# On-chip casts of the first high halves, a mask built in two parts, and constant matmuls in the early gaps of TensorE

## The chip, the cores and the metric

The kernel runs on one core of one Trainium2 chip. The metric is the device time of one execution in microseconds (us); lower is better. The engines are named as the profile names them: PE (TensorE, matmul), PEld (its weight loads), DVE (VectorE), ACT (ScalarE), POOL (GpSimd) and SP (SyncE, here only a queue that issues DMAs). PEq, ACTq, SPq and so on are the sequencers of the engines.

## The reference

Block-sparse attention over 4 batches, 8 heads, 768 positions and a head size of 64, followed by a layer norm and a two-layer feed-forward network with a residual:

```python
scores = scale * np.matmul(q, k.transpose(0, 1, 3, 2))
mask = np.abs(blk_i - blk_j) <= window          # blocks of 32 positions
mask = mask | (blk_i == 0) | (blk_j == 0) | (blk_i == n_blocks - 1) | (blk_j == n_blocks - 1)
for qb in range(n_blocks):
    for kb in sampled_blocks[qb]:                # three random blocks for each block of queries
        mask[qb * block:(qb + 1) * block, kb * block:(kb + 1) * block] = True
scores = np.where(mask, scores, -1000000000.0)
attn = np.exp(scores - np.max(scores, axis=-1, keepdims=True))
attn = attn / (np.sum(attn, axis=-1, keepdims=True) + 1e-09)
x = np.matmul(attn, v)                           # heads side by side: (4, 768, 512)
xn = (x - mu) / np.sqrt(var + 1e-06) * g_ln
out = x + np.maximum(xn @ w_ch1, 0.0) @ w_ch2    # 512 -> 2048 -> 512
```

## The kernel before

**Numbers in two halves.** An operand of a matmul that must be exact to about float32 is kept as two float16 tiles: a high half, which is the value rounded to float16, and a low half, which is the float32 value minus the high half. A product is then three float16 matmuls (high by high, low by high, high by low). For k and q the float32 original is loaded by a DMA issued on SP into `raw` (k) or `qr` (q). The high half `kh` or `qh` comes from a second DMA of the same data that converts to float16 on the way and is issued on POOL. The low half `kl` or `ql` is a subtraction: on DVE for the first k and the first q, on POOL for all the others.

**Units, segments, slots.** A unit is one batch and 256 of its 768 queries: 12 units. Each has 4 segments (pairs of heads), so there are 48 segments, each with one q load; and 16 k loads, one for each batch and pair of heads. A segment has 4 slots (2 tiles of 128 queries by 2 heads). A pair of slots is scored together: 12 float16 matmuls into two `ps` tiles (line 475). Then DVE adds the mask and takes the row extreme (`masked_max`, line 484, which reads the mask `allow`), ACT takes the exponential (line 498), and the result `p` is transposed. In the first 8 segments ("early") PE transposes it against `ident` into one of three PSUM tiles `bank` (line 512), ACT and DVE copy it to `pt` (line 519), and the product with v is made in float32 (line 588). In the other 40 segments ACT and DVE make two halves `ph` and `pl`, DMAs transpose them, and the product is in float16 (lines 592 and 597). After four segments comes the layer norm of the unit and then its feed-forward matmuls (lines 754 and 835), which work with both halves and use the same `bank` tiles.

**Weights.** The network's weights arrive as float64 bits. DVE takes three integer passes over each piece (lines 423, 427 and 431), ACT scales it and makes the high half (lines 458 and 460), POOL the low half (line 461). There are 8 pieces of the first layer (128x1024) and 16 of the second (128x512).

**The mask.** `allow` holds, for each of the 6 tiles of 128 queries, one number for each of 24 blocks of keys, and a seventh row with the block numbers. It and the sampled blocks (`samp_i`) are loaded by DMAs issued on ACT. `build_mask` is one cast, three pairs of compare and maximum, and one scaling, each over all 6 tiles (128x144 elements), all on DVE. Unit c of a batch reads tiles 2c and 2c+1.

**The planner.** The order of instructions on every engine is computed before the kernel is built. `Plan.add` records a task with its engine, a cost in ns, the tasks that it follows, a rank and the ring places that it takes or gives back. `Plan.run` plays the tasks through a list scheduler: a clock for each engine, `bus` for the DMA engines (a transfer occupies it for `load` ns), `lock` for DVE and POOL work that is kept apart, and a state `warm` for PE, in which a matmul costs its planned time, against 1.9 times that while it is not warm. Before, PE counts as warm after 4200 ns without an idle stretch over 2500 ns. A task is emitted when it is picked, so the picks are the program order of each engine. On the chip each engine works through its own list in order and waits only for the data of the next instruction. A changed cost anywhere can change the order of everything that follows. The tasks of the feed-forward matmuls have the last rank, so they fill whatever PE time attention leaves.

Of the kernel before, what the change touches and what calls it, by code (L numbers as in the profile page):

```python
# [10 lines left out]
F16 = mybir.dt.float16  # L11
# [3 lines left out]
ALU = mybir.AluOpType  # L15

NEG = -(2.0**40)
# [8 lines left out]
class Plan:  # L26
# [7 lines left out]
    LOOK = 120  # L34

    def __init__(self):
        self.tasks, self.rings, self.sets = [], {}, {}
# [7 lines left out]
    def add(self, engine, cost, emit, after=(), rank=0.0, more=100, take=(), give=(), lock=False,  # L45
            mode=None, load=None, order=None, slack=0):
        t = SimpleNamespace(engine=engine, cost=cost, emit=emit, rank=rank, more=more, take=take,
                            give=give, lock=lock, mode=mode, load=load, n=len(self.tasks),
                            after=[x for x in after if x is not None], end=None, left=0, next=[],
                            order=order, slack=slack)  # L50
# [38 lines left out]
    def where(self, name, owner):  # L89
        return (self.rings.get(name) or self.sets[name]).at[owner]  # L90

    def run(self):
        clock = dict.fromkeys(("PE", "DVE", "ACT", "POOL", "SP"), 0.0)
        held = {"DVE": 0.0, "POOL": 0.0}
        ready = {e: [t for t in self.tasks if t.engine == e and not t.left] for e in clock}
        bus, mode, done, warm, since = 0.0, None, 0, False, 0.0
        while done < len(self.tasks):
            best = None
            for e, now in clock.items():
                pick = None  # L100
                for t in ready[e]:
                    start = max([now] + [x.free if x.engine == "PE" == e or x.order == t.order
                                         and x.order else x.end + (t.slack if x.engine != e else 0)
                                         for x in t.after])
# [9 lines left out]
                    key = (max(start, now + self.LOOK), t.rank, t.n)  # L114
                    if pick is None or key < pick[0]:
                        pick = (key, start, t)
                if pick and (best is None or pick[1] < best[1]):
                    best = pick
            assert best, ("stuck", done, [(e, [(x.rank, x.take) for x in v][:6])
                                          for e, v in ready.items()])  # L120
            _, start, t = best
            ready[t.engine].remove(t)
            cost = t.cost
            if t.engine == "PE":
                if t.mode != mode:
                    start += 90
                mode = t.mode
                if start - clock["PE"] > self.idle:
                    warm, since = False, start
                warm = warm or start - since > self.heat  # L130
                if not warm:
                    cost *= 1.9
            t.free = clock[t.engine] = start + cost
# [7 lines left out]
            for name, owner in t.give:  # L141
                r = self.rings.get(name) or self.sets[name]
# [15 lines left out]
def sparse_attention_moe(  # L158
# [12 lines left out]
    nc = tc.nc  # L171
    P = 128
    B, NPAIR, NCH, _, CH = qs.shape
# [3 lines left out]
    NB = blocks.shape[2]  # L177
    NR = sampled.shape[2]
    BLK = S // NB
    KT = S // P  # L180
# [4 lines left out]
    TS = CH // P  # L185
# [4 lines left out]
    EARLYLN = 1  # L190
    EASY, EASE = 34, (0, 1500, 500)
    PORC = ()
    W1POS = (2.0, 2.0)
    W2POS = (16.0, 1.0)

# [10 lines left out]
    op = ctx.enter_context(tc.tile_pool(name="op", bufs=2))  # L206
# [4 lines left out]
    ctx.enter_context(tc.manual_schedule(engines={ET.SP, ET.Pool, ET.DVE, ET.Activation}))  # L211

    plan = Plan()
    plan.idle, plan.heat, plan.deep = 2500.0, 4200.0, 7000.0
    for name, size in (("k", 4), ("v", 4), ("vr", 2), ("q", NQ), ("qr", 3), ("ps", 2), ("p", 4),
                       ("ph", 2), ("pl", 2), ("pt", 5), ("pa", 1), ("xT", 3), ("xh", 1),
                       ("hh", 1), ("hl", 1), ("ln", 1), ("ot", 2)):
# [14 lines left out]
    eps = const.tile([P, 1], F32, name="eps")  # L232
    nc.vector.memset(eps, 1e-6)
    allow = const.tile([P, KT + 1, NB], F32, name="allow")
    nc.scalar.dma_start(allow, blocks)
    samp_i = const.tile([P, KT, 2 * NR], I32, name="samp_i")
    nc.scalar.dma_start(samp_i, sampled.bitcast(I32))
    g_sb = const.tile([P, CT], F32, name="g_sb")
    nc.scalar.add_instruction(
        mybir.InstLoadActFuncSet(  # L240
# [10 lines left out]
    w1v = w1.rearrange("(c p) f -> p c f", p=P)  # L251
    w2f, w2g = (x.rearrange("p f e -> p (f e)") for x in (w2h, w2l))

    def build_mask():
        nc.vector.tensor_copy(samp_f, samp_i.rearrange("p c (r t) -> p c r t", t=2)[:, :, :, 0])
        hit = w1h[:, CT - 1, DF - 2 * KT * NB :].bitcast(F32).rearrange("p (t n) -> p t n", n=NB)
        ids = allow[:, KT : KT + 1, :].to_broadcast([P, KT, NB])
        for r in range(NR):
            nc.vector.tensor_tensor(out=hit, in0=ids,
                                    in1=samp_f[:, :, r : r + 1].to_broadcast([P, KT, NB]),  # L260
                                    op=ALU.is_equal)
            nc.vector.tensor_tensor(out=allow[:, 0:KT], in0=allow[:, 0:KT], in1=hit, op=ALU.max)
        nc.vector.tensor_scalar(out=allow[:, 0:KT], in0=allow[:, 0:KT], scalar1=-NEG,
                                scalar2=NEG, op0=ALU.mult, op1=ALU.add)

    units, segs, slots = [], [], []
# [17 lines left out]
    def loads_k(b, pr, rank, before):  # L284
        idx = b * NPAIR + pr
# [8 lines left out]
        def low():  # L294
# [1 line left out]

        o.raw = plan.add("SP", 580, raw, (before,), rank, 1400, load=1120, order="k",
                         take=(("k", idx), ("raw", ("k", idx), 1, RAWS)))
        o.high = plan.add("POOL", 560, lambda: nc.gpsimd.dma_start(o.kh, ks[b, pr]), (o.raw,),
                          rank, 2300, load=1100, order="k")  # L300
        e, c = ("POOL", 1640) if idx else ("DVE", 960)
        o.low = plan.add(e, c, low, (o.raw, o.high), rank, give=(("raw", ("k", idx)),), lock=True)
        return o
# [1 line left out]
    def loads_q(n, rank, before):  # L305
# [3 lines left out]
        def raw():  # L309
# [7 lines left out]
        o.high = plan.add("POOL", 560, lambda: nc.gpsimd.dma_start(o.qh, qs[u.b, pr, u.c]),  # L317
                          (o.raw,), rank, 2300, load=400, order="q")
        e, c = ("POOL", 660) if n else ("DVE", 650)
        o.low = plan.add(e, c, lambda: (nc.gpsimd if n else nc.vector).tensor_sub(  # L320
            o.ql, o.qr, o.qh), (o.raw, o.high), rank, give=(("qr", n),), lock=True)
        return o
# [571 lines left out]
    for seg in segs:  # L894
# [4 lines left out]
        for t in range(TS):  # L899
# [105 lines left out]
```

## Time and profile before

| what | value |
|---|---|
| time before, median of 3 runs (lowest, highest) | 816.51 us (814.61, 822.39) |
| the profiled execution: its own time | 817.7 us |
| its span, first to last instruction | 815.9 us |
| PE busy | 779.8 us (96%) |
| DVE, ACT, POOL busy | 610.9, 514.9, 173.9 us |
| granted PE clock, mean | 0.987 |
| first score matmul; first feed-forward matmul | 7.29 us; 92.5 us |

The span is read in two stretches: the head, up to the first feed-forward matmul, in which PE waits for other engines again and again, and the rest, in which it hardly waits at all. "Idle before" in a row is the time that an engine stood still just before that instruction, with the releaser that ended it.

### The profile page before, as it was taken

The page shows a single profiled execution, that of the slowest core. Times are in us where ns is not written, and L with a number is a line of the kernel's source. Part 1 is how long each engine was busy: PE and PEld are TensorE (multiplying, and loading weights), DVE is VectorE, ACT ScalarE, POOL GpSimd, SP SyncE. Part 2 cuts the span into 40 slices and gives each one's busy share as a digit, 9 for nine tenths or more (in the row PEclk, how much of TensorE's full clock was granted, in tenths as well). Part 3 has the DMA queues.
Part 4 walks back from the last instruction along what each step waited for, and adds up shares of the span by engine and source line. Part 5 has one row for each costly group of instructions (what it writes and reads, how often), then busy time and mean ns, then how long its engine had stood idle before and what let it go on. Part 6 is the DMA issues. An engine that isn't in the chain of part 4 may idle for free.

```text
span 815.9 us, 18386 instructions
## 1 busy us (share of the span) xinstructions
PE 779.8 (96%) x7228; PEld 592.4 (73%) x7228; DVE 610.9 (75%) x1203; ACT 514.9 (63%) x942; POOL 173.9 (21%) x188
## 2 busy tenths in 40 slices
PE   4787899999999999999899999999999999999998
PEld 2454567777777867777677777777777777788887
DVE  5899988968988878868878778868869778745120
ACT  2778788668686666677666666668766656723020
POOL 4635454413211012143111012332100100000000
PEclk9799899999999999999999999999999999999999
DMA  9853424899989779999678699899697585750000
GB/s 283 289 174 95 132 70 116 159 159 207 168 155 141 130 136 168 160 193 173 124 136 141 107 152 174 168 181 169 131 144 142 107 150 101 115 107 2 27 2 27
DMA packets 293383, 112.49 MB, mean 138 GB/s; under 512 B 260400, under 2 KB 285104, under 8 KB 293296
## 3 DMA queue, kind: packets, MB, share of 16 engines
q1 hardware_dynamic: 283792, 104.91, 64.1%
q0 software_dynamic: 9216, 6.30, 6.2%
q8 instruction: 57, 0.93, 0.5%
q14 instruction: 30, 0.25, 0.1%
q10 hardware_dynamic: 288, 0.10, 0.1%
HBM read 48.34 MB, written 6.29 MB: 67 GB/s over the span
## 4 chain that ended last, share of the span: by engine, by line
PE 77%; DVE 11%; DMA 5%; ACT 4%; issue 1%; SPq 1%; ACTq 0%; DVEq 0%
PE bank L835 28%; PE bank L754 26%; PE ps L475 10%; PE pa L592 6%; DMA pt<-pl 3%; PE pa L597 3%; DVE p L484 2%; PE pa L588 2%; DVE pl L553 2%; PE bank L512 1%; ACT p L498 1%; DMA pt<-ph 1%; DVE w2h L427 1%; DMA samp_i<-sampled 1%; DMA raw<-w 1%
## 5 line engine op out<-in xcount | busy, mean ns | idle before, releaser
L498 ACT ACTIVATE p<-p,st 128x768 f32<-128x768 f32 x192 | 177.8, 926 | 43.4 <-DVE st L484 41.9
L549 ACT ACTIVATE ph<-p,st 128x768 f16<-128x768 f32 x160 | 145.3, 929 | 92.2 <-DVE st L540 42.0
L835 PE MATMUL bank<-hh,w2h 128*128 128x256 f16 x704 | 192.3, 273 | 2.5 <-DVE xc L685 2.5
L553 DVE SCALAR_TENSOR_TENSOR pl<-p,st,ph 128x768 f16<-128x768 f32 x160 | 164.3, 1038 | 38.9 <-DMA pt<-pl 37.4
L484 DVE CUSTOM_DVE_ANT_1 p<-ps,allow 128x768 f32<-128x768 f32 x192 | 178.4, 947 | 18.5 <-PE ps L475 17.4
L835 PE MATMUL bank<-hl,w2h 128*128 128x256 f16 x704 | 191.9, 273 | 0.0
L835 PE MATMUL bank<-hh,w2l 128*128 128x256 f16 x704 | 191.9, 273 | 0.0
L754 PEld LDWEIGHTS <-w1h 128*128 128x128 f16 x1536 | 146.9, 98 | 27.6 <-issue 10.7
L835 PEld LDWEIGHTS <-w2h 128*128 128x128 f16 x1408 | 134.5, 98 | 27.4 <-issue 12.4
L754 PE MATMUL bank<-xl,w1h 128*128 128x256 f16 x768 | 115.8, 274 | 0.0
L754 PE MATMUL bank<-xh,w1l 128*128 128x256 f16 x768 | 115.7, 273 | 0.0
L754 PE MATMUL bank<-xh,w1h 128*128 128x256 f16 x768 | 115.4, 273 | 0.1
L769 ACT ACTIVATE hh<-bank 128x512 f16<-128x512 f32 x96 | 56.6, 590 | 80.9 <-PE bank L754 80.2
L775 DVE SCALAR_TENSOR_TENSOR hl<-bank,hh 128x512 f16<-128x512 f32 x96 | 65.9, 686 | 35.4 <-ACT hh L769 35.1
L475 PE MATMUL ps<-kh,qh 64*128 64x256 f16 (+1 forms) x384 | 72.2, 338 | 14.2 <-DMA qh<-q 7.3
L592 PE MATMUL pa<-pt,vh 128*64 128x512 f16 x480 | 82.1, 383 | 0.7 <-issue 0.6
L754 PEld LDWEIGHTS <-w1l 128*128 128x128 f16 x768 | 73.9, 98 | 12.1 <-issue 3.8
L475 PEld LDWEIGHTS <-qh 64*128 64x128 f16 x768 | 32.5, 96 | 62.6 <-issue 28.2
L835 PEld LDWEIGHTS <-w2l 128*128 128x128 f16 x704 | 68.9, 98 | 8.0
L475 PE MATMUL ps<-kl,qh 64*128 64x256 f16 (+1 forms) x384 | 69.7, 334 | 1.4 <-DVE kl L295 1.4
L475 PE MATMUL ps<-kh,ql 64*128 64x256 f16 (+1 forms) x384 | 68.3, 334 | 1.2 <-DVE ql L320 1.2
L597 PE MATMUL pa<-pt,vl 128*64 128x256 f16 x480 | 67.4, 273 | 0.0
(106 smaller groups left out, 921.7 us busy)
## 6 DMA issues: line engine op xcount, KB each, us to landing
raw<-k SPq DMA_DIRECT2D x16, 384.0 KB, 4.6
qr<-q SPq DMA_DIRECT2D x48, 128.0 KB, 3.3
raw<-w SPq DMA_DIRECT2D x12, 512.0 KB, 3.6
out<-ot SPq DMA_DIRECT2D x48, 128.0 KB, 2.0
vr<-v SPq DMA_DIRECT2D x24, 192.0 KB, 2.9
w2l<-w SPq DMA_DIRECT2D x4, 1024.0 KB, 9.6
kh<-k POOLq DMA_DIRECT2D x16, 192.0 KB, 5.2
qh<-q POOLq DMA_DIRECT2D x48, 64.0 KB, 3.5
```

The source lines that it names most:

```text
L475: nc.tensor.matmul(s.ps[:, lo:hi], x[rows, s.qs], y[rows, lo:hi], start=n == 0, stop=n == len(terms) - 1)
L484: nc.vector.tensor_tensor_reduce(out=s.p.rearrange(blk, k=BLK), in0=s.ps[:, 0:S].rearrange(blk, k=BLK), in1=bias, scale=-0.125, scalar=3.0 ...
L498: nc.scalar.activation(s.p, s.p, AF.Exp, bias=s.st[:, j : j + 1], scale=-1.0, accum_out=total)
L549: nc.scalar.activation(s.ph, s.p, AF.Copy, scale=s.r)
L553: nc.vector.scalar_tensor_tensor(out=s.pl, in0=s.p, scalar=s.r, in1=s.ph, op0=ALU.mult, op1=ALU.subtract)
L588: nc.tensor.matmul(seg.pa[half[hh], 0:CH], vo.whole(hh)[:, t, :], pts[keys[hh]][:, t, :], start=t == 0, stop=t == KT - 1, skip_group_check ...
L592: nc.tensor.matmul(seg.pa[half[hh], 0 : 2 * CH], vo.vh[:, hh, t, :], pts[keys[hh]][:, t].rearrange("p i n -> p (i n)"), start=t == 0, stop ...
L597: nc.tensor.matmul(seg.pa[half[hh], 0:CH], vo.vl[:, hh, t, :], pts[keys[hh]][:, t, 0, :], start=False, stop=t == KT - 1, skip_group_check= ...
L754: nc.tensor.matmul(dst, w[:, ct, fs], x[:, ct, :], start=n == 0 and ct == 0, stop=n == 2 and ct == CT - 1, skip_group_check=True)
L769: nc.scalar.activation(u.hh[:, f : f + 2, :].rearrange("p f n -> p (f n)"), bank[plan.where("bank", own)], AF.Relu)
L775: nc.vector.scalar_tensor_tensor(out=u.hl[:, f : f + 2, :].rearrange("p f n -> p (f n)"), in0=bank[plan.where("bank", own)], scalar=0.0, i ...
L835: nc.tensor.matmul(dst, w[:, k, e * P : (e + 1) * P], x[:, k, :], start=k == 0 and n == 0, stop=k == FT - 1 and n == 2)
```

## The change

1. **High halves cast on chip.** For the first four k loads and the first four q loads the converting DMA on POOL is gone. The high half is now a copy from the float32 tile: on ACT for the k loads and for q loads 1 to 3, on DVE for q load 0. The planned cost of the DVE subtraction for `ql` of load 0 goes from 650 to 350 ns.
2. **The mask in two parts.** `build_mask(lo, hi)` works on a range of tiles. Part one covers tiles 0 and 1 and is a DVE task of rank 0 that is not picked before 5400 ns of the plan; part two covers tiles 2 to 5, rank 6, not before 12000 ns. A slot of the first unit of a batch waits for part one, all others for part two. `samp_i` is loaded before `allow`.
3. **Matmuls on constants.** When the planner picks a PE task that starts before 60 us of the plan, and PE's clock stands before that start, it takes the `bank` tile that comes free first and emits as many matmuls of `ones_h` by a constant (128x128 weights, 256 columns) as fit in the gap less 300 ns, counted at 115 ns each while it holds PE for warm and at 220 ns while not; under 4 it emits none. Nothing reads their result.
4. **The planner's picture of the chip.** The clocks start at 700 ns instead of 0 and `bus` at 1800 ns. PE is warm when it was busy for more than 85% of the last 3400 ns, and stays so while that is over 40%.

```diff
+    def fill(self, now, start, each):
+        free = self.sets["bank"].free
+        place = min((p for p in free if free[p] is not None), key=lambda p: free[p], default=None)
+        begin = max(now, self.first, free[place] if place is not None else start)
+        count = int((start - begin - 300) // each)
+        if count >= 4:
+            self.filler(place, count)
+            free[place] = begin + each * count + 200
+            self.work.append((begin, begin + each * count))
...
-        clock = dict.fromkeys(("PE", "DVE", "ACT", "POOL", "SP"), 0.0)
+        clock = dict.fromkeys(("PE", "DVE", "ACT", "POOL", "SP"), 700.0)
...
-        bus, mode, done, warm, since = 0.0, None, 0, False, 0.0
+        bus, mode, done, warm = 1800.0, None, 0, False
...
+            if t.engine == "PE" and start < self.keep:
+                self.fill(clock["PE"], start, 115 if warm else 220)
...
-                if start - clock["PE"] > self.idle:
-                    warm, since = False, start
-                warm = warm or start - since > self.heat
+                part = sum(max(0, b - max(a, start - self.span)) for a, b in self.work[-60:])
+                part /= self.span
+                warm = part > self.hot or warm and part > self.cold
...
+    KEEP = 60e3
+    CASTK, CASTQ = 4, 4
...
-    plan.idle, plan.heat, plan.deep = 2500.0, 4200.0, 7000.0
+    plan.span, plan.hot, plan.cold, plan.deep = 3400.0, 0.85, 0.4, 7000.0
+    plan.keep, plan.first = KEEP, 1400.0
...
-    nc.scalar.dma_start(allow, blocks)
     samp_i = const.tile([P, KT, 2 * NR], I32, name="samp_i")
     nc.scalar.dma_start(samp_i, sampled.bitcast(I32))
+    nc.scalar.dma_start(allow, blocks)
...
+    def filler(place, count):
+        for _ in range(count):
+            nc.tensor.matmul(bank[place][:, 0 : 2 * P], ones_h, ones.bitcast(F16), start=True,
+                             stop=True)
...
-    def build_mask():
+    def build_mask(lo, hi):
+        ts, n = slice(lo, hi), hi - lo
...
-        o.high = plan.add("POOL", 560, lambda: nc.gpsimd.dma_start(o.kh, ks[b, pr]), (o.raw,),
-                          rank, 2300, load=1100, order="k")
+        if idx < CASTK:
+            o.high = plan.add("ACT", 900, lambda: nc.scalar.copy(o.kh, o.kr), (o.raw,), rank)
+        else:
+            o.high = plan.add("POOL", 560, lambda: nc.gpsimd.dma_start(o.kh, ks[b, pr]),
+                              (o.raw,), rank, 2300, load=1100, order="k")
...
+        if n < CASTQ:
+            o.high = plan.add("ACT" if n else "DVE", 310 if n else 200, lambda: (
+                nc.scalar.copy if n else nc.vector.tensor_copy)(o.qh, o.qr), (o.raw,), rank)
...
-    mask = plan.add("DVE", 2300, build_mask, (), -2000, 100)
-    mask.more = 4000
+    masks = [plan.add("DVE", 1250, lambda: build_mask(0, TS), (), 0, 100),
+             plan.add("DVE", 2100, lambda: build_mask(TS, KT), (), 6, 100)]
+    masks[0].wake, masks[1].wake = 5400.0, 12000.0
...
-                last_m = plan.add("DVE", 880, lambda s=s: masked_max(s), (sc, mask, last_m),
+                last_m = plan.add("DVE", 880, lambda s=s: masked_max(s), (sc, masks[u.c > 0], last_m),
```

More of the change, by code (lines that the diff above doesn't have):

```diff
@@ L36, in __init__ @@
     def __init__(self):
-        self.tasks, self.rings, self.sets = [], {}, {}
+        self.tasks, self.rings, self.sets, self.work = [], {}, {}, []
     def ring(self, name, size):
@@ L49, in add @@
                             after=[x for x in after if x is not None], end=None, left=0, next=[],
-                            order=order, slack=slack)
+                            order=order, slack=slack, wake=0.0)
         for x in t.after:
@@ L101, in run @@
                 for t in ready[e]:
-                    start = max([now] + [x.free if x.engine == "PE" == e or x.order == t.order
+                    start = max([t.wake] + [x.free if x.engine == "PE" == e or x.order == t.order
                                          and x.order else x.end + (t.slack if x.engine != e else 0)
@@ L114, in run @@
                     key = (max(start, now + self.LOOK), t.rank, t.n)
+                    start = max(start, now)
                     if pick is None or key < pick[0]:
@@ L127, in run @@
                 mode = t.mode
-                if start - clock["PE"] > self.idle:
-                    warm, since = False, start
-                warm = warm or start - since > self.heat
+                part = sum(max(0, b - max(a, start - self.span)) for a, b in self.work[-60:])
+                part /= self.span
+                warm = part > self.hot or warm and part > self.cold
                 if not warm:
                     cost *= 1.9
+                self.work.append((start, start + cost))
             t.free = clock[t.engine] = start + cost
@@ L252, in sparse_attention_moe @@
     w2f, w2g = (x.rearrange("p f e -> p (f e)") for x in (w2h, w2l))
-    def build_mask():
-        nc.vector.tensor_copy(samp_f, samp_i.rearrange("p c (r t) -> p c r t", t=2)[:, :, :, 0])
+    def filler(place, count):
+        for _ in range(count):
+            nc.tensor.matmul(bank[place][:, 0 : 2 * P], ones_h, ones.bitcast(F16), start=True,
+                             stop=True)
+    plan.filler = filler
+    def build_mask(lo, hi):
+        ts, n = slice(lo, hi), hi - lo
+        nc.vector.tensor_copy(samp_f[:, ts],
+                              samp_i.rearrange("p c (r t) -> p c r t", t=2)[:, ts, :, 0])
         hit = w1h[:, CT - 1, DF - 2 * KT * NB :].bitcast(F32).rearrange("p (t n) -> p t n", n=NB)
-        ids = allow[:, KT : KT + 1, :].to_broadcast([P, KT, NB])
+        hit = hit[:, ts]
+        ids = allow[:, KT : KT + 1, :].to_broadcast([P, n, NB])
         for r in range(NR):
             nc.vector.tensor_tensor(out=hit, in0=ids,
-                                    in1=samp_f[:, :, r : r + 1].to_broadcast([P, KT, NB]),
+                                    in1=samp_f[:, ts, r : r + 1].to_broadcast([P, n, NB]),
                                     op=ALU.is_equal)
-            nc.vector.tensor_tensor(out=allow[:, 0:KT], in0=allow[:, 0:KT], in1=hit, op=ALU.max)
-        nc.vector.tensor_scalar(out=allow[:, 0:KT], in0=allow[:, 0:KT], scalar1=-NEG,
+            nc.vector.tensor_tensor(out=allow[:, ts], in0=allow[:, ts], in1=hit, op=ALU.max)
+        nc.vector.tensor_scalar(out=allow[:, ts], in0=allow[:, ts], scalar1=-NEG,
                                 scalar2=NEG, op0=ALU.mult, op1=ALU.add)
@@ L316, in loads_q @@
                          take=(("q", n), ("qr", n)))
-        o.high = plan.add("POOL", 560, lambda: nc.gpsimd.dma_start(o.qh, qs[u.b, pr, u.c]),
-                          (o.raw,), rank, 2300, load=400, order="q")
-        e, c = ("POOL", 660) if n else ("DVE", 650)
+        if n < CASTQ:
+            o.high = plan.add("ACT" if n else "DVE", 310 if n else 200, lambda: (
+                nc.scalar.copy if n else nc.vector.tensor_copy)(o.qh, o.qr), (o.raw,), rank)
+        else:
+            o.high = plan.add("POOL", 560, lambda: nc.gpsimd.dma_start(o.qh, qs[u.b, pr, u.c]),
+                              (o.raw,), rank, 2300, load=400, order="q")
+        e, c = ("POOL", 660) if n else ("DVE", 350)
         o.low = plan.add(e, c, lambda: (nc.gpsimd if n else nc.vector).tensor_sub(
```

## The prediction

> **What bounds the kernel now.** I read first the slices of the page, then the busy time of each engine by stretch, cut at the events that matter: first matmul, first masked maximum, the end of the loaded DMA stretch, 60 us (where the constant matmuls stop), and the first feed-forward matmul.
>
> ```profile
> PEclk9799899999999999999999999999999999999999
> DMA  9853424899989779999678699899697585750000
> ```
> ```profile
> 0.00:7.28 7.28, 0.00 (x0) 0.00 (x0) 1.62 (x8) 1.28 (x1) 3.55 (x11) 1.00 0.81 211
> 7.28:12.31 5.03, 2.46 (x12) 0.81 (x13) 3.59 (x6) 0.00 (x0) 3.54 (x4) 1.00 1.08 295
> 12.31:35.00 22.69, 17.48 (x102) 10.60 (x101) 18.37 (x29) 13.11 (x22) 10.30 (x9) 0.77 1.05 340
> 35.00:60.00 25.00, 20.97 (x161) 12.40 (x159) 23.19 (x45) 20.48 (x37) 11.77 (x10) 0.93 0.51 168
> 60.00:92.40 32.40, 25.27 (x190) 15.68 (x186) 28.96 (x59) 26.16 (x53) 15.79 (x11) 0.95 0.38 115
> 92.40:110.00 17.60, 15.95 (x133) 10.96 (x133) 17.44 (x31) 15.28 (x30) 10.62 (x10) 0.90 0.31 83
> 110.00:815.90 705.90, 697.71 (x6643) 541.91 (x6642) 517.75 (x1029) 438.55 (x802) 118.35 (x136) 1.00 0.73 131
> ```
>
> The columns of the second fence are the stretch, its length, busy time of PE, PEld, DVE, ACT and POOL with instruction counts, granted clock, DMA share, GB/s. After 110 us PE is busy 697.71 of 705.9 us: PE bounds it, 8.2 us are idle, and the change puts nothing there but another order. In the head PE isn't the bound: from 12.31 to 92.4 us it is busy 63.7 of 80.1 us, DVE 70.5. DVE is the fullest engine, and the transfers are saturated to 35 us. So the end moves with the head: PE work done there comes off the end one for one, and the head goes at the pace of DVE and, where DVE stands idle, of what it waits for.
>
> **The first chain.** Timeline rows (start, duration, engine and line), in brackets the idle time before:
>
> ```profile
> 0.75 0.40 SPq L292 DMA_DIRECT2D raw<-k  x1
> 1.20 0.42 SPq L313 DMA_DIRECT2D qr<-q  x1
> 1.66 0.42 SPq L292 DMA_DIRECT2D raw<-k  x1
> 5.83 0.18 DVE L255 CAST samp_f<-samp_i 128x18 f32<-128x18 int32 x1 [4.68 <-DMA samp_i<-sampled]
> 7.29 0.61 PE L475 MATMUL ps<-kh,qh 64*128 64x512 f16 x2 [7.29 <-DMA qh<-q]
> 8.25 0.95 DVE L295 TENSOR_TENSOR kl<-raw,kh 128x768 f16<-128x768 f32 x1
> 8.77 1.92 POOL L295 TENSOR_TENSOR kl<-raw,kh 128x768 f16<-128x768 f32 x1 [4.30 <-DMA kh<-k]
> 9.12 1.86 DVE L320 TENSOR_TENSOR ql<-qr,qh 128x256 f16<-128x256 f32 x1
> 11.03 0.61 PE L475 MATMUL ps<-kh,ql 64*128 64x512 f16 x2 [1.17 <-DVE ql L320]
> 11.90 4.21 SPq L292 DMA_DIRECT2D raw<-k  x1
> 12.31 0.96 DVE L484 CUSTOM_DVE_ANT_1 p<-ps,allow 128x768 f32<-128x768 f32 x1 [1.34 <-PE ps L475]
> 14.22 1.00 PE L475 MATMUL ps<-kl,qh 64*128 64x512 f16 x2
> 14.62 1.02 PE L475 MATMUL ps<-kh,ql 64*128 64x512 f16 x2
> ```
>
> The mask holds DVE from 5.83 to 8.25 us, ahead of `kl`; `ql`, a third of the size of `kl`, takes twice as long, and ends 0.3 us after POOL's own `kl`. The first masked maximum, from which DVE, ACT and PE live, starts at 12.31. For the new chain I need landings and durations. Of the DMA issues (last figure: us to landing), in narrow windows, these are the first k, the first q, the second and the fourth k; behind them stand nearest rows for the new operations (count, busy us, mean ns):
>
> ```profile
> raw<-k SPq DMA_DIRECT2D x1, 384.0 KB, 3.5
> qr<-q SPq DMA_DIRECT2D x1, 128.0 KB, 3.5
> ...
> raw<-k SPq DMA_DIRECT2D x1, 384.0 KB, 5.2
> ...
> raw<-k SPq DMA_DIRECT2D x1, 384.0 KB, 15.1
> ...
> L338 ACT CAST vh<-vr 128x384 f16<-128x384 f32 x2 | 0.9, 512 | 0.0
> L460 ACT CAST w1h<-w2h 128x1024 f16<-128x1024 f32 x8 | 8.4, 1048 | 0.2
> L519 DVE COPY pt<-bank 128x256 f32<-128x256 f32 x23 | 9.4, 417 | 1.2 <-PE bank L512 1.2
> L685 DVE TENSOR_TENSOR xc<-xT,bank 128x256 f32<-128x256 f32 x4 | 1.4, 412 | 0.0
> L259 DVE TENSOR_TENSOR w1h<-allow,samp_f 128x144 f32<-128x144 f32 x3 | 0.9, 308 | 0.1
> ```
>
> The first k lands at 0.75 + 3.5 = 4.25, the first q at 4.70. ACT, free by then, casts 128x768, between the rows of 512 and 1048 ns: 512 + 536 x 384/640 = 0.83, so `kh` is there at 5.1. DVE copies q (at most 0.42), subtracts `ql` (0.41), and at 5.5 `kl` (0.95): 6.5. PE needs 1.28 us after `ql` today (11.03 to 12.31), and 0.40 more for the group with `kl`, the spacing of the rows at 14.22 and 14.62: 8.2. Part one of the mask, 8 instructions: a third of the 2.4 us if cost goes by elements, all of it if by instructions. Between the 176 ns of 18 elements and the 308 ns of 144, 48 elements take 0.21; with 0.035 between starts, six of them and the cast and scaling make 1.8. DVE is through at 8.3 and the first maximum could start at 8.4. But POOL's `kl` of the second k now starts at about 7.7 (its raw tile lands at 1.66 + 5.2 = 6.9, cast 0.83), beside the end of the mask. If that holds DVE as it held `ql`, the start is at 9.6; if not, at 8.4. The value I take is the middle, 9.0: **3.3 us earlier** (2.7 to 3.9).
>
> The Trainium skill, page "SBUF — State Buffer", section "Who interferes with whom", speaks against the change here: a DVE instruction with two SBUF inputs and a GpSimd instruction that reads SBUF exclude each other for a whole instruction. The trace agrees for `ql` (1.86 us, ending just behind POOL's 1.92). By the rule this term would be 2.7 us.
>
> **What is added on DVE.** Part two of the mask: 96 elements give 0.26 + 0.035, six times, with cast and scaling 2.2 us. It costs nothing if it falls into an idle stretch of DVE, 2.2 if it pushes everything behind it. DVE idles twice for about 2 us before 35 us (rows below), but the integer passes want the same gaps: I take half, **1.1 us later**.
>
> **The clock.** The page grants 1.00 before 20 us, but durations say otherwise:
>
> ```profile
> 15.05 0.42 PE L475 MATMUL ps<-kh,qh 64*128 64x256 f16 x1
> 16.14 0.96 DVE L484 CUSTOM_DVE_ANT_1 p<-ps,allow 128x768 f32<-128x768 f32 x1 [1.98 <-PE ps L475]
> 34.48 0.42 DVE L618 TENSOR_TENSOR xT<-pa,xT 128x256 f32<-128x256 f32 x1 [2.05 <-ACT xT L615]
> 37.16 0.27 PE L475 MATMUL ps<-kh,qh 64*128 64x256 f16 x1
> ```
> ```profile
> 14.21 2.07 PE ps L475 x10
> 29.97 3.62 PE pa L588 x24
> 57.04 2.74 PE pa L588 x24
> 65.23 1.15 PE ps L475 x10
> ```
>
> The same matmul takes 0.42 us at 15 us and 0.27 at 37; in the chain of work (second fence: start, time, what) ten score matmuls take 2.07 against 1.15, 24 of the product with v 3.62 against 2.74. So PE runs slow until about 32 us. Constant matmuls from about 1.4 us on should end that before the second pair. It shows only where DVE waits for PE: the 1.98 us before 16.14 shorten by 2.07 - 1.15 = 0.9, the 2.05 before 34.48 by 3.62 - 2.74 = 0.9. **1.8 us earlier**; nothing if PE stays slow, and 3.4 if two more stretches that DVE covers today (another ten scores, six transposes) come to count.
>
> The Trainium skill, "TensorE: Matmul & The Clock Gate", section "What's actually happening", has a free-running window of about 3.4 us that must be busy. The trace agrees in kind: with 17.48 of 22.69 us busy the clock rose late. A block of constant matmuls from 1.4 us with the scores behind it would hold one such window.
>
> **The constant matmuls' own cost.** Idle PE between 7.28 and 60 us is 2.6 + 5.2 + 4.0 = 11.8 us, and the batches are sized to fit into the planner's picture of it. The cover is that next inputs on the chip come no sooner than planned; the rows run somewhat over the planned costs (masked maximum 0.96 against 0.88, copy 0.42 against 0.335), so I take nothing. Without that cover see the slower rival.
>
> **Transfers and ACT.**
>
> ```profile
> q0 software_dynamic: 9216, 6.30, 6.2%
> ```
>
> The converting DMAs took 6.2% of 815.9 us, 50.6 us. Four k (192 KB) and four q (64 KB) of 16 and 48 are a sixth of the bytes: 8.4 us less in a stretch where the DMA share is 1.05. First weights then land sooner, and DVE can fill with them what is left of the gap before 16.14 (1.98 - 0.9 = 1.1): between 0 and 1.1, taken as the middle, **0.6 us earlier**. POOL loses eight issues and gains nothing. ACT gains three casts of 0.83 and three of up to 0.5 besides the first: 4 us, under its 9.6 idle of 12.31 to 35; without that cover, 4 us later. What waits on ACT now is the cast for the raw tile, with exponentials and `pt` copies queued behind.
>
> **Sum.** 3.3 - 1.1 + 1.8 + 0.6 = 4.6 us. Against the profiled execution's own 817.7 (span 815.9 and 1.8 around it) that is 813.1; that execution was 1.2 above the median of 816.51, so on the median's scale the forecast is **811.9 us**. The new order after 110 us can give or take a few of the 8.2 idle us there; I take nothing, and 3 as its bound.
>
> **Rivals.**
> - *More than the sum.* All terms at their better ends: 3.9 + 0 + 3.4 + 1.1 = 8.4 us, 808.1; a lucky order behind adds up to 3: 805. For it: DVE idles 9.6 us between 12.31 and 92.4, and part of it is PE's slowness. Against: DVE is about 90% busy from 35 us on, and takes the same passes.
> - *Swallowed.* The start is earlier, but ACT stands before late raw tiles (the fourth k landed at 11.90 + 15.1 = 27 us), exponentials behind it wait, and DVE's passes reach the first feed-forward matmul no sooner: 815 to 818. Or PE never speeds up, so that the change doesn't do what it says: 811.9 + 1.8 = 813.7.
> - *Slower.* One mechanism: PE takes its queue in order, and a batch counted at 115 ns runs at 0.2 us each (half the 0.40 of 512 columns before 20 us) where the chip's PE is slow while the planner holds it for fast. All 11.8 us of gaps, filled that way, overrun by three quarters of themselves, some 9 us; with the 1.8 not gained, that is 811.9 + 11 = 823. It decides from the point where a batch outlasts the wait of the instruction behind it; a batch that waits for the last reader of its `bank` tile does the same. Half of it gives 818.
>
> **Chances.** One per cent (8.2 us) is about what a measurement of this kernel can tell from no change: under 808.3 is faster, over 824.7 slower. The forecast, 808.3 to 814.5: 0.48. More than the sum, under 808.3: 0.20. Swallowed, 814.5 to 818: 0.20. Slower than before, over 818: 0.12, half of it over 824.7. So faster 0.20, same 0.74, slower 0.06. With a tenth left out on each side the range is 804.5 to 819.5.
>
> **What would show it.** First masked maximum near 9.0 us; `ql` near 0.4 us; the 256-column score matmul at 0.27 instead of 0.42 us before 20 us; the mask's instructions at about 0.21 and 0.26 us; the first feed-forward matmul near 88 us instead of 92.5; PE busy up by the constant matmuls alone. I would be wrong if the head ends at the same time in spite of an earlier start, if PE waits behind constant matmuls, or if the idle time after 110 us changes by more than 3 us.

## The result and the profile after

The changed kernel is slower: 822.21 us (median of 19 runs, 818.43 to 825.29) against 816.82 us of the kernel before in the same session (19 runs), a ratio of 1.0062 with a 95% interval of 1.0044 to 1.0079. The profiled execution took 823.44 us, its span is 821.6 us: 5.7 us more than before.

The busy time by stretch, with the columns of the prediction's second fence:

```profile
0.00:7.28 7.28, 5.75 (x34) 3.62 (x35) 2.75 (x10) 3.56 (x5) 1.23 (x7) 1.00 0.73 229
7.28:12.31 5.03, 2.24 (x20) 1.62 (x20) 4.60 (x9) 0.99 (x3) 2.37 (x3) 1.00 1.00 341
12.31:35.00 22.69, 17.88 (x130) 11.98 (x130) 20.23 (x36) 14.67 (x26) 10.55 (x7) 0.88 0.74 264
35.00:60.00 25.00, 22.54 (x181) 14.49 (x180) 23.18 (x38) 19.04 (x31) 10.13 (x8) 0.91 0.60 190
60.00:92.40 32.40, 25.19 (x181) 15.34 (x182) 28.57 (x57) 25.78 (x51) 15.10 (x12) 0.95 0.39 108
92.40:110.00 17.60, 16.15 (x136) 12.27 (x135) 16.13 (x32) 13.00 (x27) 8.07 (x7) 0.90 0.23 68
110.00:821.60 711.60, 699.73 (x6641) 541.46 (x6638) 523.13 (x1035) 442.51 (x811) 118.78 (x139) 1.00 0.72 130
```

The last row splits the loss. After 110 us PE is busy 699.73 us, against 697.71 before, 2.0 us more. And PE is idle 711.6 - 699.7 = 11.9 us there, against 8.2: 3.7 us more. 2.0 + 3.7 = 5.7. But most of the 2.0 us isn't work that the head left over. From 237.6 to 241.0 us the granted clock (the third figure from the right) is 0.50, just after PE stood idle for 1.23, 0.96 and 0.26 us, and the 256-column score matmul is back at 0.42 us:

```profile
237.60:241.00 3.40, 3.35 (x18) 1.43 (x18) 2.26 (x5) 2.01 (x4) 0.00 (x0) 0.50 0.44 101
236.81 0.57 PE L789 MATMUL bank<-xh,w1h 128*128 128x256 f16 x2 [0.96 <-ACT xh L766]
240.06 0.42 PE L510 MATMUL ps<-kh,qh 64*128 64x256 f16 x2
```

The kernel before has no such stretch between 110 us and its end. My estimate of what it costs is half of PE's 3.35 us there, 1.7 us. That leaves 0.3 us: the head came out level with the one before, not ahead, and the loss lies behind it. Two numbers of a kernel, PE busy after 110 us and idle PE after it, are used below; where the first contains stretches at half clock, it is said.

The first chain in the timeline of the kernel after (start, duration, engine and line; in brackets the idle time before):

```profile
4.17 0.83 ACT L328 CAST kh<-raw 128x768 f16<-128x768 f32 x1 [1.22 <-DMA raw<-k]
4.71 0.29 DVE L349 CAST qh<-qr 128x256 f16<-128x256 f32 x1 [3.55 <-DMA qr<-q]
5.03 0.43 DVE L355 TENSOR_TENSOR ql<-qr,qh 128x256 f16<-128x256 f32 x1
5.38 0.95 DVE L323 TENSOR_TENSOR kl<-raw,kh 128x768 f16<-128x768 f32 x1
6.68 0.21 DVE L290 TENSOR_TENSOR allow<-allow,w1h 128x48 f32<-128x48 f32 x1
6.75 1.65 POOL L323 TENSOR_TENSOR kl<-raw,kh 128x768 f16<-128x768 f32 x1 [5.43 <-ACT kh L328]
6.93 1.53 DVE L287 TENSOR_TENSOR w1h<-allow,samp_f 128x48 f32<-128x48 f32 x1
8.36 1.29 POOL L355 TENSOR_TENSOR ql<-qr,qh 128x256 f16<-128x256 f32 x2
8.49 0.59 DVE L290 TENSOR_TENSOR allow<-allow,w1h 128x48 f32<-128x48 f32 x1
9.12 0.59 DVE L287 TENSOR_TENSOR w1h<-allow,samp_f 128x48 f32<-128x48 f32 x1
10.32 0.96 DVE L519 CUSTOM_DVE_ANT_1 p<-ps,allow 128x768 f32<-128x768 f32 x1
```

Up to the end of `kl` all is as worked out. Then the same mask instruction takes 0.21 us where POOL is idle and 1.53 and 0.59 us while POOL subtracts. The same happens to the other part of the mask, and to an integer pass later:

```profile
19.92 0.75 DVE L281 CAST samp_f<-samp_i 128x12 f32<-128x12 int32 x1
21.04 2.21 POOL L496 TENSOR_TENSOR w1l<-w2h,w1h 128x1024 f16<-128x1024 f32 x1 [0.40 <-ACT w1h L495]
21.29 2.07 DVE L287 TENSOR_TENSOR w1h<-allow,samp_f 128x96 f32<-128x96 f32 x1
23.40 0.26 DVE L290 TENSOR_TENSOR allow<-allow,w1h 128x96 f32<-128x96 f32 x1
24.27 0.21 DVE L291 TENSOR_SCALAR allow<-allow 128x96 f32<-128x96 f32 x1
27.23 2.08 POOL L323 TENSOR_TENSOR kl<-raw,kh 128x768 f16<-128x768 f32 x1 [3.34 <-ACT kh L328]
27.85 2.54 DVE L466 SCALAR_TENSOR_TENSOR w2h<-w1r,w2h 128x1024 int32<-128x1024 int32 x1
```

Part two holds DVE from 19.92 to 24.48, 4.56 us, of which 0.6 + 1.8 = 2.4 are above what the same instructions take elsewhere. The constant matmuls made PE fast, but not for the pair that needed it:

```profile
5.66 0.39 PE L510 MATMUL ps<-kh,qh 64*128 64x512 f16 x2
7.25 1.81 PE L274 MATMUL bank<-ones,ones_h 128*128 128x256 f16 x15
11.34 0.37 PE L510 MATMUL ps<-kh,qh 64*128 64x512 f16 x1 [2.29 <-DVE st L519]
13.03 0.42 PE L510 MATMUL ps<-kh,qh 64*128 64x256 f16 x1
14.10 0.96 DVE L519 CUSTOM_DVE_ANT_1 p<-ps,allow 128x768 f32<-128x768 f32 x1 [1.93 <-PE ps L510]
```

The first pair runs at full speed (0.39 for 512 columns, 0.61 before). The batch behind it ends at 9.06; the mask is late, PE stands idle for 2.29 us, and at 13 us the score matmul is back at 0.42. DVE waits 1.93 us for the second pair, as it did before (1.98).

### The profile page after: what moved, and what is told of

The parts are those of the page before. It is cut to its first block, busy times and chain, and to the rows that moved or that the text cites. A ratio compares the mean times of both kernels' runs of the same rounds, so it can differ in the third digit from the quotient of the medians.

```text
span 821.6 us, 18556 instructions
## 1 busy us (share of the span) xinstructions
PE 789.5 (96%) x7311; PEld 600.8 (73%) x7311; DVE 618.6 (75%) x1212; ACT 519.5 (63%) x949; POOL 166.2 (20%) x180
## 4 chain that ended last, share of the span: by engine, by line
PE 68%; DVE 16%; DMA 8%; ACT 6%; issue 2%; SPq 0%; ACTq 0%; DVEq 0%
PE bank L789 24%; PE bank L870 23%; PE ps L510 9%; PE pa L627 5%; DMA pt<-pl 5%; DVE p L519 3%; DVE pl L588 3%; PE pa L632 2%; DMA pt<-ph 2%; ACT p L533 2%; PE bank L547 2%; ACT ph L584 1%; PE pa L623 1%; DVE w2h L466 1%; DVE hl L810 1%
## 5 line engine op out<-in xcount | busy, mean ns | idle before, releaser
L588 DVE SCALAR_TENSOR_TENSOR pl<-p,st,ph 128x768 f16<-128x768 f32 x160 | 166.3, 1051 | 29.3 <-DMA pt<-pl 26.7
L510 PE MATMUL ps<-kh,qh 64*128 64x256 f16 (+1 forms) x384 | 67.3, 334 | 6.4 <-DVE st L519 6.4
L510 PE MATMUL ps<-kl,qh 64*128 64x256 f16 (+1 forms) x384 | 66.3, 331 | 0.3 <-DVE kl L323 0.3
L510 PE MATMUL ps<-kh,ql 64*128 64x256 f16 (+1 forms) x384 | 65.9, 331 | 0.0
```

What stands on the lines that cost most here:

```text
L510: nc.tensor.matmul(s.ps[:, lo:hi], x[rows, s.qs], y[rows, lo:hi], start=n == 0, stop=n == len(terms) - 1)
L588: nc.vector.scalar_tensor_tensor(out=s.pl, in0=s.p, scalar=s.r, in1=s.ph, op0=ALU.mult, op1=ALU.subtract)
```

## The experiments

Two theories were put against each other. The mask: its instructions wait for POOL, and that holds the head. The order: the planner's new order of the tasks costs time by itself.

**Without the constant matmuls** (`a_nofill`: the changed kernel's order, `range(0)` for `range(count)` in `filler`).

> The changed kernel in its own order, with the 83 constant matmuls left out and nothing else changed. If they cost time (PE stands behind them while its next input is there), the time falls by up to the 9.7 us that PE spends on them, to 813 to 820. If they do what they are for (a PE that runs fast early), the score matmuls before 20 us go back to 0.42 us and the time rises by 1 to 3 us over the changed kernel, to about 824. If the head is paced by DVE (the mask and the integer passes), it stays within 1 us of the changed kernel's 822, which is what I expect.

Measured: 822.86 us, ratio 1.0064 (1.0040 to 1.0089): no difference from the changed kernel's 1.0062. In its trace the first pair is slow, the first maximum where it was:

```profile
5.01 0.61 PE L510 MATMUL ps<-kh,qh 64*128 64x512 f16 x2 [5.01 <-ACT kh L328]
10.31 0.96 DVE L519 CUSTOM_DVE_ANT_1 p<-ps,allow 128x768 f32<-128x768 f32 x1
```

So the 83 matmuls neither cost nor gain as far as the times can tell; the two intervals leave some 2.5 us either way, more than the 1.8 us that I had put on the clock. The rows say why: the first maximum starts at 10.31 us without them and at 10.32 with them, and DVE's wait for the second pair is 1.96 and 1.93 us. What they speed up waits for the mask anyway. My slower rival, PE behind its own constant matmuls, whose overrun I had priced at some 9 us, falls.

**Without part two of the mask** (`a_nopart2`, same order):

```diff
-             plan.add("DVE", 2100, lambda: build_mask(TS, KT), (), 6, 100)]
+             plan.add("DVE", 2100, lambda: None, (), 6, 100)]
```

> The changed kernel in its own order, with the eight instructions of the mask's part two left out (the scores of tiles 2 to 5 get the unscaled mask). Theory of the mask: part two holds DVE from 19.92 to 24.48 us, 4.56 us of its full stretch, and all of that comes off the head: first feed-forward matmul 3 to 4.5 us earlier, time 817.5 to 819. Rival, the order: the loss is made after 110 us by another order of the tasks, and then the time stays within 1.5 us of the changed kernel's 822.

Measured: 817.91 us, ratio 1.0002 (0.9986 to 1.0019) against 1.0062, which is 4.9 us; first feed-forward matmul at 86.9 us instead of 92.0. Within the noise all 4.56 us of part two lie on the path.

**Part two in the first gap** (`a_part2_early`): part two follows the second masked maximum instead of a time of the plan, and goes ahead of everything else that is ready.

```diff
-             plan.add("DVE", 2100, lambda: build_mask(TS, KT), (), 6, 100)]
-    masks[0].wake, masks[1].wake = 5400.0, 12000.0
+             plan.add("DVE", 2100, lambda: build_mask(TS, KT), (), -2000, 100)]
+    masks[0].wake = 5400.0
...
+                if s.i == 1:
+                    masks[1].after.append(last_m)
...
```

> The changed kernel with the mask's part two placed right behind the first two masked maxima, where DVE stands idle for 1.93 us and POOL has nothing to do until 19 us. The planner makes a new order from there. Theory of the mask: its eight instructions run without waiting for POOL, 2.1 us, nearly all of it in that gap, and the time falls by about 4 us to 818. Theory of the order: any new order moves the time by some 3 to 5 us either way, and then this is anywhere from 813 to 827, with idle PE after 110 us well away from the 11.9 us of the changed kernel.

Measured: 830.12 us, ratio 1.0143 (1.0115 to 1.0172). Part two did what was wanted:

```profile
12.39 0.17 DVE L281 CAST samp_f<-samp_i 128x12 f32<-128x12 int32 x1
13.18 0.26 DVE L287 TENSOR_TENSOR w1h<-allow,samp_f 128x96 f32<-128x96 f32 x1
14.35 0.21 DVE L291 TENSOR_SCALAR allow<-allow 128x96 f32<-128x96 f32 x1
...
110.00:831.20 721.20, 704.77 (x6632) 548.12 (x6632) 523.12 (x1031) 439.07 (x806) 117.97 (x137) 0.99 0.71 128
```

Eight instructions in 2.2 us, none held; and yet PE is busy for 704.8 us after 110 us (some 3.4 of them lost to two stretches at half clock) and idle for 16.4. The expectation for the mask missed: a mended mechanism in a new order lost 0.8% more, some 6.6 us. From here on a run was judged only within one order, or over several orders.

**POOL's subtractions beside the mask replaced** (`a_nopool`, same order; the low halves of k loads 1 and 2, q loads 1 and 2 and the first piece of weights are zero):

```diff
-            (nc.gpsimd if idx else nc.vector).tensor_sub(o.kl, o.kr, o.kh)
+            if idx in (1, 2):
+                nc.gpsimd.memset(o.kl, 0.0)
+            else:
+                (nc.gpsimd if idx else nc.vector).tensor_sub(o.kl, o.kr, o.kh)
...
```

The subtractions for `ql` and for the piece of weights are replaced by `memset` in the same way.

> The changed kernel in its own order, with POOL's subtractions beside the two parts of the mask (the low halves of the second and third k, of q loads 1 and 2, and of the first piece of weights) replaced by writes of zeros, which read nothing; these low halves are then zero. If POOL holds the mask's instructions, the ones of 1.53, 0.59 and 2.07 us fall to 0.21 and 0.26, part one ends 2 us earlier, near 8.2, and part two takes 2.2 instead of 4.4 us; with both on the path the time falls by 2 to 4.5 us, to 818 to 820. If those durations have another reason, they stay, and the time is 822.

Measured: 815.35 us, ratio 0.9992 (0.9962 to 1.0022).

```profile
7.59 0.21 DVE L290 TENSOR_TENSOR allow<-allow,w1h 128x48 f32<-128x48 f32 x1
8.17 0.96 DVE L522 CUSTOM_DVE_ANT_1 p<-ps,allow 128x768 f32<-128x768 f32 x1
11.13 0.96 DVE L522 CUSTOM_DVE_ANT_1 p<-ps,allow 128x768 f32<-128x768 f32 x1 [1.12 <-PE ps L513]
18.05 0.17 DVE L281 CAST samp_f<-samp_i 128x12 f32<-128x12 int32 x1
20.01 0.21 DVE L291 TENSOR_SCALAR allow<-allow 128x96 f32<-128x96 f32 x1
```

The compares and maxima of the mask are at 0.21 us in part one and 0.26 in part two, the first maximum at 8.17, and part two takes 2.2 us. With the first maximum on time PE is still fast for the second pair (256 columns in 0.27 us), and DVE's wait for it falls to 1.12. The gain, 0.7% or 5.7 us, is more than the 4.5 us I had allowed; POOL also has less to do, which this run doesn't separate.

**POOL made to wait for the mask** (`a_wait`, same order, all work kept): POOL copies 24 elements of each finished part of the mask before its first subtraction of k and of weights.

```diff
+            if idx == 1:
+                nc.gpsimd.tensor_copy(seen[:, 0], allow[:, TS - 1])
             (nc.gpsimd if idx else nc.vector).tensor_sub(o.kl, o.kr, o.kh)
...
+            if own == (1, 0):
+                nc.gpsimd.tensor_copy(seen[:, 1], allow[:, KT - 1])
+            nc.gpsimd.tensor_sub(o.dl, o.src, o.dh)
```

> The changed kernel in its own order and with all of its work; POOL copies 24 elements of the finished mask before its first subtraction (second k) and again before its first subtraction of weights, so that these two wait until each part of the mask is done, instead of the mask for them. If POOL's hold on the mask is what the change lost, this gets most of what the zeroed halves got: first masked maximum near 8.2, part two in 2.2 to 2.8 us, time 816 to 819. If the delayed subtractions cost as much as the mask gains, or if the zeroed halves gained for another reason (less POOL work), it stays near the changed kernel's 822.

Measured: 819.53 us, ratio 1.0030 (0.9998 to 1.0061), half of the loss by the medians. Its interval overlaps that of the changed kernel, so the time alone doesn't show a gain; the rows show what moved.

```profile
8.13 0.96 DVE L526 CUSTOM_DVE_ANT_1 p<-ps,allow 128x768 f32<-128x768 f32 x1
16.72 1.14 DVE L282 CAST samp_f<-samp_i 128x12 f32<-128x12 int32 x1
19.64 0.21 DVE L292 TENSOR_SCALAR allow<-allow 128x96 f32<-128x96 f32 x1
20.65 1.59 DVE L962 TENSOR_SCALAR nm<-nm 128x4 f32<-128x4 f32 x1
20.08 2.14 POOL L502 TENSOR_TENSOR w1l<-w2h,w1h 128x1024 f16<-128x1024 f32 x1
```

Part one is free, and DVE's wait for the second pair is 1.12 us here too, with all the work kept. Part two is held once more, at its cast (1.14 us, beside the subtraction of the third k, which doesn't wait), and takes 3.1 us instead of 4.6. What comes next is held instead: four elements in 1.59 us, beside POOL's 2.14.

**Orders exchanged at 110 us of the plan** (`s_after_before`: the changed kernel's head, behind it on every engine the order of the kernel before; `s_before_after`: the reverse).

> The changed kernel up to 110 us of the planner's clock; from there on every engine takes the remaining tasks in the order in which the kernel before takes them. Theory of the order: the 3.7 us of extra idle PE after 110 us (11.9 against 8.2) come from the new order there, and go: idle after 110 us near 8, time about 818. Theory of the mask: the head alone is late, and what follows is its echo; idle after 110 us stays near 12 and the time within 1.5 us of the changed kernel's 822.

> The reverse: the kernel before up to 110 us of the planner's clock, then the changed kernel's order of the remaining tasks. Theory of the order: idle PE after 110 us rises from 8.2 to about 12, time 820. Theory of the mask: nothing changes, 816 to 818.

Measured: 829.73 us, ratio 1.0170 (1.0122 to 1.0219), and 826.52 us, ratio 1.0131 (1.0089 to 1.0174). Both theories missed: idle PE after 110 us is 15.0 and 12.7 us, more than either kernel has with its own order behind its own head. It looks as if an order fits only its own head; whether the changed kernel's is good can't be read from this.

**Neutral orders.** One planned cost moved by 4 ns (score matmuls at 1004 or 996 instead of 1000); the instructions are the same, their order isn't.

> The changed kernel with one planned cost moved by 4 ns (the twelve score matmuls at 1004 instead of 1000); no instruction is added or taken away, only the order that the planner finds differs. Theory of the order: the time scatters, by 2 us or more from the changed kernel's 822, either way. Theory of the mask: since the split mask stays on DVE's path, the time stays within 1.5 us of 822.

> The changed kernel with 996 instead of 1000 ns. Its first neutral order (1004) was 7 us slower than the changed kernel. If the changed kernel's order is an average one, this is as likely below 822 as above; if its order was a good one too, it is again slower, 824 to 830.

> The kernel before with the planned cost of the twelve score matmuls at 1004 instead of 1000 ns: the same instructions in another order. If the order alone is worth one per cent here too, it comes out 3 to 10 us from the kernel before, and rather slower, since that is the order that was chosen. If the kernel before is not sensitive, within 2 us.

> The same with 996 ns: a second neutral order of the kernel before. Order: 3 to 10 us away, rather slower; no sensitivity: within 2 us.

**Kinds of kernel in several orders.** `b_casts` is the kernel before with the on-chip casts alone, `a_whole` the changed kernel with one whole mask first on DVE; two more kernels add one piece of the planner's new picture to the casts.

> The kernel before with the on-chip casts alone: whole mask first on DVE, no constant matmuls, the old picture in the planner. Part by part: the mask still ends at about 8.2 us, ql takes 0.4 instead of 1.86 us, and the first masked maximum starts at about 11.0 instead of 12.31. Theory of the mask (the casts are good, the split mask is what costs): 1 to 2 us faster than before, 815. If the casts cost (ACT stands before late k tiles): 818 to 821. Theory of the order: 812 to 822, and the difference sits after 110 us.

> The kernel before with the casts alone, second order (1004 ns). If the casts are worth something, the middle of their three orders is below that of the kernel before (816.8, 821.5, 824.2; middle 821.5) by 2 to 6 us, so 812 to 820 here. If they cost: 820 to 828.

> The kernel before with the casts alone, third order (996 ns). As for the second: 812 to 820 if the casts gain, 820 to 828 if they cost.

> The changed kernel with the mask in one piece, first on DVE as in the kernel before; casts, constant matmuls and the planner's new picture stay. First masked maximum near 11 us (mask to 8.2, then q, ql, kl and the scores). If the split mask is the loss, this kind is faster than the changed one: 4 us over three orders (822.2, 829.0, 832.0; middle 829), so 812 to 826 for one order. If the loss is in the other parts, it is like the changed kernel: 822 to 832.

> The same with the score matmuls planned at 1004 ns. If the split mask is the loss: 812 to 826, and the middle of the three orders at least 4 us below the changed kernel's 829. If not: 822 to 832.

> The kernel before with the casts, and the planner's clocks starting at 700 and its transfers at 1800 ns; one whole mask, old rule for a fast PE, no constant matmuls. If the start makes the slow orders: ratio 1.010 to 1.017, 824 to 830, first feed-forward matmul near 90 us again. If not: like the casts alone, 0.998 to 1.004, first feed-forward matmul near 78 us.

> The kernel before with the casts and the planner's new rule for a fast PE (busy over 85% of 3400 ns), old start, one whole mask, no constant matmuls, so that more early PE work is planned at 1.9 times its cost. If the rule makes the slow orders: ratio 1.010 to 1.017. If not: 0.998 to 1.004.

All of them in one table. "Half clock" is my estimate of what PE lost after 110 us at a granted clock of 0.50, half of its busy time there; it is part of the column before it. "Held" is DVE time in the first 110 us beyond the usual: for each DVE instruction, what it takes above the lower quartile of the same operation and size in the first 110 us of all these kernels, where that is over 0.15 us. Apart from the ratio, a row comes from one profiled execution, and executions of one kernel differ (the changed kernel's from 818.4 to 825.3 us).

| kernel | ratio to before (95%) | PE busy after 110 us | half clock | idle PE after 110 us | DVE held |
|---|---|---|---|---|---|
| before, 1000 | 1 | 697.7 | 0 | 8.2 | 8.0 |
| before, 1004 | 1.0040 (1.0013 to 1.0067) | 697.5 | 0 | 9.6 | 6.8 |
| before, 996 | 1.0090 (1.0053 to 1.0128) | 700.2 | 1.5 | 12.9 | 6.1 |
| casts alone, 1000 | 0.9986 (0.9958 to 1.0014) | 691.9 | 0 | 11.1 | 7.2 |
| casts alone, 1004 | 1.0032 (1.0001 to 1.0062) | 694.0 | 0 | 11.6 | 8.8 |
| casts alone, 996 | 1.0038 (1.0005 to 1.0071) | 694.1 | 1.6 | 10.7 | 7.8 |
| changed, 1000 | 1.0062 (1.0044 to 1.0079) | 699.7 | 1.7 | 11.9 | 10.7 |
| changed, 1004 | 1.0169 (1.0114 to 1.0223) | 701.3 | 1.7 | 16.5 | 13.1 |
| changed, 996 | 1.0166 (1.0114 to 1.0218) | 703.8 | 3.0 | 16.5 | 11.3 |
| changed, whole mask, 1000 | 1.0163 (1.0098 to 1.0229) | 705.4 | 4.7 | 15.0 | 12.5 |
| changed, whole mask, 1004 | 1.0150 (1.0075 to 1.0225) | 700.7 | 0 | 11.4 | 13.4 |
| casts and later start of the clocks | 1.0218 (1.0166 to 1.0269) | 701.3 | 0 | 15.5 | 13.9 |
| casts and new rule for a fast PE | 1.0150 (1.0104 to 1.0196) | 703.3 | 0 | 12.9 | 14.0 |
| changed, no part two | 1.0002 (0.9986 to 1.0019) | 693.6 | 0 | 11.0 | 9.6 |
| changed, POOL's reads replaced | 0.9992 (0.9962 to 1.0022) | 696.5 | 1.6 | 10.8 | 6.5 |
| changed, POOL waits | 1.0030 (0.9998 to 1.0061) | 697.1 | 0 | 11.0 | 10.5 |

What follows:

- A neutral order moves either kernel by 0.4 to 1.1%. In both kinds the order that was submitted is the fastest of its three. So is the first order of the casts alone, which was not picked from several, so with three orders of each this can be chance.
- The kernel before isn't always held. `n_before`, `n2_before` and `s_before_after` have the same DVE order up to the first maximum. In their traces `samp_i` landed 0.8 us earlier than in the trace that I predicted from, `ql` was through before POOL began, and the first maximum started at 10.1 us, not at 12.31. These are the rows of `n_before`:

```profile
8.32 0.42 DVE L320 TENSOR_TENSOR ql<-qr,qh 128x256 f16<-128x256 f32 x1
8.81 1.64 POOL L295 TENSOR_TENSOR kl<-raw,kh 128x768 f16<-128x768 f32 x1 [4.32 <-DMA kh<-k]
10.14 0.96 DVE L484 CUSTOM_DVE_ANT_1 p<-ps,allow 128x768 f32<-128x768 f32 x1 [1.40 <-PE ps L475]
```

- An earlier first maximum doesn't carry through to the end of the head. `s_before_after` has the head of the kernel before and starts it 2.2 us earlier; its first feed-forward matmul is at 92.2 instead of 92.5 us.
- The casts alone put the head ahead: 692 to 694 us of PE time left against 698 to 700, first feed-forward matmul at 77.8 instead of 92.5 us (80.3 and 77.7 in the other two orders). Their first maximum, though, starts at 13.0 us in all three, not at 11.0 as I had expected: POOL holds the last steps of the whole mask (one takes 1.67 us instead of 0.31). Of the 5 us ahead the time keeps little: the mean ratio is 1.0019 against 1.0043 for the three orders of before, single runs overlap, and the middle one is 0.7 us lower, not 2 to 6. Idle PE after 110 us is 11 us in all three.
- The split mask isn't what separates the changed kernel from the casts: with one whole mask it is no faster (1.0163, 1.0150). My expectation for `a_whole` was wrong; POOL holds `ql` there instead (1.74 us), and the first maximum starts at 12.2 us. What goes with the slow kernels is the planner's new picture: either piece of it, added to the casts, gives 1.015 to 1.022. Each piece was measured in one order only, but all eight kernels that have a piece of it, an order of their own and all of their work (the changed kernel in three orders and with a whole mask in two, `a_part2_early`, and these two) are slower, 1.006 to 1.022, than the casts alone in any order, 0.999 to 1.004.
- The slow kernels have DVE held for longer. In the kernel with the later start it shows in the integer passes, which take 0.69 and 1.22 us elsewhere:

```profile
21.31 2.13 DVE L431 TENSOR_SCALAR w2h<-w1r 128x1024 int32<-128x1024 int32 x1
23.47 3.34 DVE L435 SCALAR_TENSOR_TENSOR w2h<-w1r,w2h 128x1024 int32<-128x1024 int32 x1
...
21.24 1.65 POOL L296 TENSOR_TENSOR kl<-raw,kh 128x768 f16<-128x768 f32 x1 [11.15 <-ACT kh L301]
23.58 2.14 POOL L469 TENSOR_TENSOR w1l<-w2h,w1h 128x1024 f16<-128x1024 f32 x1
```

Over these sixteen kernels together with `a_nofill` (11.8 us held) and `a_part2_early` (11.3), but without the two with exchanged orders, time and held DVE time go together (correlation 0.80, 1.8 us for each us held). That is a correlation, and the kernel before at 996 is an exception (slow with 6.1 us held). Shown by taking the cause away, in one order, is only what `a_nopart2` and `a_nopool` gained.

No kernel with all of its work beat both: the best, the casts alone, is level with the kernel before (0.9958 to 1.0014).

## Why the prediction was wrong, by its own steps

- **First chain, 3.3 us earlier: 2.0 measured** (12.31 to 10.32). Casts, `ql` (0.43), `kl` and the unhindered mask (1.8 us, first maximum at 8.17 in `a_nopool`, 8.4 forecast) were right. The term that was mis-sized is the hold by POOL: I let one instruction wait, and took half of it, 0.6 us; three waited, 1.3 + 0.4 + 0.4 = 2.1 us. The page "SBUF — State Buffer" of the Trainium skill, section "Who interferes with whom", by whose rule I had worked out 2.7 us for this term, was the better guide: two DVE inputs in SBUF against a reading POOL exclude each other, here 1.53 us beside 1.65. Even it was applied to one subtraction only, where three came in a row. The 12.31 to start from was itself a held execution: against the 10.1 us of the three other traces of that head, the changed kernel gained nothing.
- **Part two, 1.1 us later (0 to 2.2): 4.6 measured,** outside my bounds. I had bounded it by its own length and forgot to ask for the second part what I had asked for the first: which POOL work runs beside it. The hold is 2.4 of the 4.6 us. With part two left out the kernel is 4.9 us faster, by the ratios.
- **The clock, 1.8 us earlier: nothing.** PE was fast at 5.66 us as forecast, and slow again at 13. The step took the speed as kept once reached; the late mask opened a gap of 2.29 us behind the batch. The trace before had shown that it isn't kept: there 512 columns take 0.39 us at 19.78 us, and 0.61 at 22.08, after 1.92 us idle, so PE was not slow all the way to 32 us. Of the two waits that I priced at 0.9 us each, the first stayed (1.98 and 1.93 us); in `a_nopool` and `a_wait`, where the mask is on time, it falls by 0.8, so there the mechanism was right. The second is gone, but in `a_nofill` too, so not by the constant matmuls.
- **Transfers, 0.6 us: nothing in the gap.** The first raw weights did land earlier (at 11.4 instead of 14.6 us), in time for the gap. But the first integer pass stands behind the third masked maximum in both orders (14.98 and 17.02 us), so the gap before the second pair stayed 1.93 us.
- **The sum and the head.** I let the start of the chain move the end of the head one for one. Neither 4.6 us ahead, as forecast, nor what the measured terms give, 2.0 - 4.6 or 2.6 us behind, came out: the head is level to 0.3 us. What made up for the late part two is not told apart; without it the head is 4.2 us ahead (693.6 against 697.7).
- **The new order, taken as nothing with 3 us as its bound: 3.7 us of idle PE,** and some 1.7 us more at half clock behind such idle time. This is nearly all of the loss, and the step that was furthest off in kind. The neutral orders show 0.4 to 1.1%, 3 to 9 us, from nothing at all; my whole sum was 4.6 us, and the range had no room for them. What in the orders makes them slow is only partly told by the held DVE time; the rest stays open, and so does why either piece of the new picture leads the planner to such orders.
- **Signs and rivals.** Two of the three signs of being wrong that I had named came true: the head ended at the same time in spite of an earlier start, and the idle time after 110 us changed by more than 3 us. The slower rival had the right sign and the wrong mechanism. DVE held by POOL stood in the text for part one alone, as an uncertainty of a term and never as a rival with a price.

## What to carry to other kernels

Where two engines exclude each other, a new DVE task needs a check against all work that the other engine has planned for that time, at every place where the task is put, and the planner must know it as well as it knows the rest. In a kernel ordered by a list scheduler, the order is a change of its own: measure a few neutral orders first, and don't credit or blame an edit for less than they scatter. Compare kinds over several orders, or edits within one frozen order. Before a forecast starts from a row, see whether that row is the same in another execution. And busy time is not work: look at the granted clock before reading one as the other.

## What the runs showed of the hardware beyond what was expected

A DVE instruction on four elements (128x4) took 1.59 us beside POOL's subtraction and 0.16 us otherwise, and a cast of 12 elements 0.75 instead of 0.17: size is no protection. Where the traces record a granted clock of 0.50 inside the span, the stretch lasts 3.41 us or two or three times that, in all twenty kernels; the changed kernel has one as late as 237.6 us, after some 2.5 us of idle PE in three pieces. PE, fast at 7.25 us, was slow again at 13.03 after one idle stretch of 2.29 us. The Trainium skill, "TensorE: Matmul & The Clock Gate", section "Why this matters for your kernels", advises against idle gaps over about 3 us; here a shorter one, with one matmul of 0.37 us in the next 0.9 us, was enough.
